# First MLP layer in seven half-block products for six pairs of feature blocks, positions worked parity by parity

## The chip, the core and the metric

The kernel runs on one core of a Trainium2 chip. The metric is the time of one execution on the device in microseconds (us), as the median of the runs of a kernel. A profile of one execution shows what each engine did: PE is TensorE (matrix products), DVE is VectorE, ACT is ScalarE, POOL is GpSimd, SP issues transfers (DMAs).

## The reference

A gated mix of two branches over 2048 positions of width 640: attention over eight positions at a distance of two (32 heads of 20 features), and an MLP with Mish of inner width 1728. Both read the same `x`.

```python
g = _sigmoid((x * gate_w).sum(-1, keepdims=True))
# branch A: idx = pos - 2 * (0..7), masked below 0
qkv = x @ wqkv
logits = jnp.einsum("bhsd,bhswd->bhsw", q, kg) * scale
o = jnp.einsum("bhsw,bhswd->bhsd", _softmax(logits), vg)
a = o @ wo
# branch B
h = jnp.einsum("bsd,df->bsf", x, w1) + b1
act = h * jnp.tanh(softplus(h))
b = jnp.einsum("bsf,fd->bsd", act, w2)
return g * a + (1 - g) * b
```

## The kernel before

**Precision and products.** Every fp32 operand is split into a high part (a copy on ACT, L373) and a low part (a subtraction on DVE or POOL, L376), and every product is three matmuls into one accumulation in a PSUM bank (`mm3`, L405 to L410): high by high, high by low, low by high. A split tile is called `pair`. There are seven banks for products, and an eighth, `side`, for the attention.

**Tiling.** Positions are laid out as 128 partitions by 16 slots. A slot belongs to one of two parities P (a window reaches back in steps of two, so attention stays in one parity), and the 2048 positions form four token blocks `tb` of 512, two for each parity. The width of 640 is five chunks `kc` of 128. The 1728 features of the MLP are 13 blocks `fc` of 128 and a rest of 64.

**First stage.** Eight units u = (quarter of the heads, parity), parity changing fastest, each make q, k and v for eight slots of 128 positions (`qkv`, L568): 15 matmuls of 496 columns for a slot. The result goes by ACT (`qkv_evac`, L558: L561, L563, L565) from the bank to one of two buffers, `kvq0` and `kvq1` in turn, the last unit to a third, `kvq2`, where six tiles of `x` lay before. Between the units stand the 52 blocks of the first MLP layer (`mlp1`, L698): for one feature block and one token block, 15 matmuls of 512 columns into a bank, then bias and Mish on ACT (L670), then stores to DRAM.

**Attention.** It runs on DVE (`attention`, L441), unit after unit, in two halves of four slots: scores (L461, L464), softmax (its exponential on ACT, L486), weighted sum (L503 to L512), and a turn (L416, `ot`) that ends the half. A buffer `kvq` may be overwritten by the unit after next only behind the turn of its half (`freed`). ACT copies q to `side` ahead of the scores (L467).

**Second stage.** The second MLP layer (`mlp2`, L869) is already made of seven products, a, b, c, e, g, d, f, over token-block pairs and weight sums. Behind product a its four `p` banks are copied by ACT (`copy`, L885) to places in `kvq1`, which is allowed only when the attention of unit 5 is over (`free5`); product b then goes on accumulating in the same banks, and its first matmul into each must wait for the copy. Then `wo_out` multiplies the attention's output by `wo`; its last part, chunks 3 and 4 of token blocks 2 and 3, is 60 matmuls.

**Order.** A list scheduler (`Plan`, L59) walks through all tasks with a cost for each, and writes one fixed instruction order for each engine. Tasks marked "ANY" (low parts of splits, sums) go to POOL or DVE; DVE takes one when PE needs it soon (`due`, L120). PE's tasks keep the order in which they are added. On the chip each engine works through its order strictly, and waits on semaphores.

## Time and profile before

| | |
|---|---|
| median of 3 runs | 637.5 us (635.89 to 637.86) |
| the profiled execution's own time | 636.0 us |
| its span, first to last instruction | 634.2 us |
| instructions | 8574 |
| moved by DMA | 136.49 MB, mean 215 GB/s |
| HBM read, written | 76.85 MB, 57.02 MB |

The span is what the profile divides up; 1.8 us of the execution's own time lie around it. A busy share is an average over stages with different limits, so a change is judged in the stage that it touches: the first stage runs to about 400 us, the second to the end.

### The profile page before, as it was taken

Reading aid. Unit: us, or ns where it says so; the run is one execution under the profiler, and the core shown is the slowest. Engines: PE = TensorE matmul, PEld = TensorE weight load, DVE = VectorE, ACT = ScalarE, POOL = GpSimd, SP = SyncE. Lnnn points to the kernel's source line nnn. Section 1 sums busy time; section 2 is a strip of 40 time slices with the busy share of each in tenths; the row PEclk is TensorE's granted clock in tenths of the full one; section 3 lists DMA queues with packets and bytes.
Section 4 is the critical chain, followed back from the end, with each engine's and each line's share of the span. In section 5 each row is a group of like instructions: output and inputs, shape, how many; then the busy total and the mean of one; then the engine's idle time right before and its main releaser. Section 6 shows DMA issues by size and latency. Waiting matters only on the chain.

```text
span 634.2 us, 8574 instructions
## 1 busy us (share of the span) xinstructions
PE 628.9 (99%) x2789; PEld 523.3 (83%) x2789; DVE 535.4 (84%) x524; ACT 334.2 (53%) x744; POOL 187.9 (30%) x179
## 2 busy tenths in 40 slices
PE   9999999999999999999999999999999999999997
PEld 6888888888888888888888888888888888888885
DVE  6589969999996999999799879999999999984230
ACT  7785753436436432443634245765687645674224
POOL 2667334333203230222242224444315613000000
PEclk9999999999999999999999999999999999999999
DMA  8999999859923994699499936898988677976204
GB/s 318 380 329 188 269 166 289 246 147 288 253 76 94 276 237 89 200 203 206 93 276 232 215 81 188 247 260 235 303 272 303 201 225 233 269 263 211 84 0 166
DMA packets 91085, 136.49 MB, mean 215 GB/s; under 512 B 12176, under 2 KB 41232, under 8 KB 91008
## 3 DMA queue, kind: packets, MB, share of 16 engines
q1 hardware_dynamic: 83360, 122.04, 62.2%
q0 software_dynamic: 7680, 13.90, 14.7%
q8 instruction: 22, 0.36, 0.2%
q14 instruction: 23, 0.19, 0.1%
HBM read 76.85 MB, written 57.02 MB: 211 GB/s over the span
## 4 chain that ended last, share of the span: by engine, by line
PE 97%; DMA 1%; ACT 1%; POOL 0%; issue 0%; DVE 0%; SPq 0%; ACTq 0%
PE bank L410 32%; PE bank L409 32%; PE bank L408 32%; PE bank L555 1%; DMA b<-kvq 1%; PE bank L357 1%; POOL pair L376 0%; PE bank L987 0%; PE bank L986 0%; ACT kvq L885 0%; ACT bank L885 0%; ACT kvq L1061 0%; DVE lg L353 0%; SPq L382 0%; ACTq L1061 0%
## 5 line engine op out<-in xcount | busy, mean ns | idle before, releaser
L409 PE MATMUL bank<-pair 128*128 128x512 f32 (+1 forms) x460 | 177.6, 386 | 0.1
L410 PE MATMUL bank<-pair 128*128 128x512 f32 (+1 forms) x460 | 177.5, 386 | 0.0
L408 PE MATMUL bank<-pair 128*128 128x512 f32 (+1 forms) x460 | 177.5, 386 | 0.0
L376 POOL TENSOR_TENSOR pair<-raw,pair 128x512 fp32r<-128x512 f32 (+2 forms) x47 | 58.7, 1266 | 148.2 <-ACT pair L373 39.8
L409 PEld LDWEIGHTS bank<-pair 128*128 128x128 f32 x460 | 86.3, 188 | 17.1 <-POOL pair L376 0.5
L408 PEld LDWEIGHTS bank<-pair 128*128 128x128 f32 x460 | 86.3, 188 | 16.5
L461 DVE TENSOR_TENSOR pr<-kvq,side 128x2560 f32<-128x2560 f32 x32 | 90.2, 2818 | 11.6 <-ACT side L467 11.2
L410 PEld LDWEIGHTS bank<-pair 128*128 128x128 f32 x460 | 86.3, 188 | 16.4
L499 DVE TENSOR_TENSOR pr<-kvq,side 128x2560 f32<-128x2560 f32 x32 | 90.3, 2820 | 1.1
L464 DVE TENSOR_REDUCE lg<-pr 128x128 f32<-128x2560 f32 x32 | 90.2, 2818 | 0.9
L561 ACT ACTIVATE kvq<-bank 128x320 f32<-128x320 f32 x64 | 28.2, 441 | 114.0 <-PE bank L410 114.0
L373 ACT ACTIVATE pair<-raw 128x512 fp32r<-128x512 f32 (+2 forms) x113 | 66.1, 612 | 13.6 <-DMA raw<-actt 8.5
L408 PE MATMUL bank<-pair,kvq 128*128 128x512 f32 (+1 forms) x188 | 72.6, 386 | 0.0
L409 PE MATMUL bank<-pair,kvq 128*128 128x512 f32 (+1 forms) x188 | 72.6, 386 | 0.0
L410 PE MATMUL bank<-pair,kvq 128*128 128x512 f32 (+1 forms) x188 | 72.6, 386 | 0.0
L670 ACT ACTIVATE hb<-bank,bias 128x512 f32<-128x512 f32 x52 | 35.8, 688 | 67.5 <-PE bank L410 59.2
L408 PE MATMUL bank<-pair,w 128*128 128x512 f32 x182 | 70.8, 389 | 0.0
L409 PE MATMUL bank<-pair,w 128*128 128x512 f32 x182 | 70.8, 389 | 0.0
L410 PE MATMUL bank<-pair,w 128*128 128x512 f32 x182 | 70.8, 389 | 0.0
L376 DVE TENSOR_TENSOR pair<-raw,pair 128x512 fp32r<-128x512 f32 (+2 forms) x66 | 46.9, 725 | 18.9 <-ACT pair L373 18.9
L658 POOL DMA_DIRECT2D actt<-actt x28 | 25.6, 964 | 87.3 <-issue 25.5
L509 DVE TENSOR_TENSOR pr<-pr 128x1280 f32<-128x1280 f32 x32 | 49.5, 1547 | 0.9
(103 smaller groups left out, 923.0 us busy)
## 6 DMA issues: line engine op xcount, KB each, us to landing
actt<-hb SPq DMA_DIRECT2D x52, 256.0 KB, 4.8
act<-hb SPq DMA_DIRECT2D x38, 256.0 KB, 4.1
raw<-actt SPq DMA_DIRECT2D x31, 256.0 KB, 4.1
raw<-act SPq DMA_DIRECT2D x27, 256.0 KB, 4.0
actt<-hb POOLq DMA_DIRECT2D x26, 256.0 KB, 6.4
actt<-actt POOLq DMA_DIRECT2D x24, 256.0 KB, 5.7
hb<-actt SPq DMA_DIRECT2D x23, 256.0 KB, 3.6
kvq<-in_xt SPq DMA_DIRECT2D x16, 320.0 KB, 7.1
```

What stands on the lines that cost most here:

```text
L373: a = add("ACT", act_ns(n), lambda: A.activation(hi(), raw(), AF.Copy), after, rank=rank, take=take, hold=hold)
L376: return (V if e == "DVE" else G).tensor_tensor(lo(), raw(), hi().bitcast(F32), op=OP.subtract)
L408: nc.tensor.matmul(ps, ah, bh, start=first, stop=False, skip_group_check=more)
L409: nc.tensor.matmul(ps, ah, bl, start=False, stop=False, skip_group_check=more)
L410: nc.tensor.matmul(ps, al, bh, start=False, stop=last, skip_group_check=more)
L461: return V.tensor_tensor(pr, window(kv, s0, 0), qs[:, :, None, :].to_broadcast([128, 2, W, QF]), op=OP.mult)
L464: return V.tensor_reduce(lg_w[:, s0:s0 + 2], pr.rearrange("p s w (h d) -> p s w h d", d=DH), op=OP.add, axis=AX.X)
L499: return V.tensor_tensor(pr.rearrange("p s w (h d) -> p s w h d", d=DH), vw, pw[:, :, :, :, None].to_broadcast([128, 2, W, HQ, DH]), op=OP ...
L509: step("DVE", 1495, lambda: V.tensor_tensor(pr[:, :, 0:4], pr[:, :, 0:4], pr[:, :, 4:8], op=OP.add))
L561: a = add("ACT", 330, lambda: A.activation(kv[:, 7 + s], ps.t[:, QF:3 * QF].rearrange("p (a b) -> p a b", a=2), AF.Copy), [done] + before, ...
L658: return add("POOL", 1200, lambda: G.dma_start(out=blk[key][:rows], in_=src(), accum_op=OP.add, max_dma_last_dim=2048), after, rank=-0.5, ...
L670: a = add("ACT", 595, lambda: A.activation(to(it()), src(), AF.Mish, bias=bias[:n, fc:fc + 1]), after + [bias_in], rank=NEXT, take=[] if h ...
```

## The change

Feature blocks q and q + 7 (q from 0 to 5) are taken together with the two token blocks of a parity, and chunks 0 to 3 of the width in two halves: two by two blocks, whose product takes seven half products instead of eight (the Winograd form of Strassen's). The fifth chunk is multiplied as before and added to the same banks. Feature block 6 stays as it was (`mlp1`).

- `quad(q, P, R)` does one such group on PE: 14 chunk products and 4 for the fifth chunk, 54 matmuls, where four calls of the old `mlp1` make 60. Five banks are used; shared part sums go from bank to bank, and to a tile `z`, by ACT (`copy` in `quad`, four a group). The two blocks of feature q + 7 are ended on DVE by adding `z` to the bank (`closed`, two a group), and Mish then reads the tile.
- `sums_of_x(P)` loads eight tiles of `x` again, makes four sums of tokens for each half and splits them. `weights_of(q, again)` makes the sums of weights, stores them, and for parity 1 loads and splits them again.
- Units are now u = 4 P + quarter: all of parity 0, then all of parity 1. `wq` is loaded and split for each parity anew, `x` of parity 1 comes only with its units (`x2`, `y3`).
- The order of PE's work is a string, `FRONT` for the first stage and `BACK` for steps inside `mlp2` (sums of `w2`, the rest of the features, gates, `wo`). Splits of `wo` go to `pair` tiles. In the scheduler POOL may begin work when DVE is free, and ACT puts off an exponential while a group is open.

In the order of PE 2800 rows become 2728 (one row a matmul; nine loads, and one branch, belong to the start).

```diff
+SIZES = {"pair": 23, "home": 6, "raw": 9, "hb": 4, "z": 2}
+FRONT = """q1 s0 w0 Q00 Q01 Q10 F0 r00 F1 Q11 g1 r10 T00 q2 T10 r20 Q20 r30 T20 r40 Q21 q3 T30 T40 Q30 r50
+w1 y3 q4 T50 x2 s1 Q31 F2 r01 Q40 M0 M1 F3 T01 S0 r11 r21 T11 q5 r31 Q41 T21 Q50 r41 S3 S1
+q6 T31 S2 Q51 T41 Q60 r51 T51 Q61 q7 H S4 Q70 Q71"""
+BACK = "40W 37P0 39P1 48P4 19G 4S6 0M2 0M3 0S5"
...
-                        if on:
+                        if on and busy["DVE"] and now < quiet:
+                            fit = [t for t in fit if t.kind != "plus" or now - t.rdy > self.STAY] or fit
+                        if on and busy["DVE"]:
...
+                        if self.open > 0:
+                            fit = [t for t in fit if t.kind != "exp" or now - t.rdy > self.HELD]
...
+    def sums_of_x(P):
+        early = EARLY_S * P
+
+        t0, t1 = 2 * P, 2 * P + 1
+        for kp in range(2):
+            raws = {}
+            for tb, kc in ((t1, 2 * kp), (t1, 2 * kp + 1), (t0, 2 * kp), (t0, 2 * kp + 1)):
+                raws[tb - t0, kc - 2 * kp] = raw = raw_buf()
+                raw.ready = [dma(lambda raw=raw: raw.t, lambda tb=tb, kc=kc: x[tb, kc], take=[raw])]
...
+            s1 = sum_into((a22, 0), (a21, 0), (a22, 0), OP.add, a21.ready + a22.ready + a22.read, 512, early=early)
+            s3 = sum_into((a21, 0), (a11, 0), (a21, 0), OP.subtract, [s1] + a11.ready + a21.read, 512, early=early)
+            s2 = sum_into((a11, 0), (a22, 0), (a11, 0), OP.subtract, [s3] + a11.read, 512, early=early)
+            s4 = sum_into((a12, 0), (a12, 0), (a11, 0), OP.subtract, [s2] + a12.ready + a12.read, 512, early=early)
+            for i, raw, t in ((1, a22, s1), (2, a11, s2), (4, a12, s4), (3, a21, s3)):
+                XS[kp, i] = halved(raw, [t], home_buf() if i < 4 else None)
...
+    def weights_of(q, again):
+
+        fa, fb = q, q + KH
...
+        if again:
+            return [load_pair(lambda: w1[fa][:, :4], "ANY", cols=4)] + [load_pair(lambda i=i: t_d[q, i], "ANY", after=t_in[q, i]) for i in range(1, 4)]
...
+        s1 = sum_into((r[2], 0), (r[1], 0), (r[0], 0), OP.subtract, [d0, d1], 256, take=[r[2]])
+        d3 = add("SP", 900, fifth, [s1], take=[r[3]], size=131072)
+        s2 = sum_into((r[2], 256), (r[1], 256), (r[2], 0), OP.subtract, [s1], 256)
+        s3 = sum_into((r[1], 0), (r[1], 256), (r[1], 0), OP.subtract, [s2], 256)
+        s4 = sum_into((r[3], 0), (r[0], 256), (r[2], 256), OP.subtract, [s2, d3], 256)
...
+    def quad(q, P, R):
+
+        fa, fb, t0, t1 = q, q + KH, 2 * P, 2 * P + 1
+        one, five, two_, three, four = ps_buf(), ps_buf(), ps_buf(seeded=True), ps_buf(seeded=True), ps_buf(seeded=True)
+        z5, z12 = z_buf(), z_buf()
...
+        p1 = mm(one, of(xs(t0, 0), 0, 0), [], True, True, [one], "open")
+        p5 = mm(five, of(s(1), 2, 0), [p1], True, True, [five])
+        c2 = copy(two_, one, [p1])
+        c5 = copy(z5, five, [p5])
+        p6 = mm(two_, of(s(2), 2, 256), [p5, c2])
+        p2 = mm(one, of(xs(t0, 1), 0, 256) + [(X[t0, 4], R[3], 256)], [p6, c2], False, True)
+        mish(lambda: one.t, 128, fa, t0, [p2], [one])
+        c3 = copy(three, two_, [p6])
+        p7 = mm(two_, of(s(3), 1, 0), [p2, c3])
+        c4 = copy(four, two_, [p7], "shut")
+        p3 = mm(three, of(s(4), 1, 256) + [(X[t0, 4], R[3], 384)], [p7, c3], False, True)
+        p4 = mm(two_, of(xs(t1, 1), 3, 0) + [(X[t1, 4], R[3], 256)], [p3, c4], False, True)
+        p8 = mm(four, [(X[t1, 4], R[3], 384)], [p4, c4], False, True)
...
+        a = closed(three, z12, [p3, c5], [z12])
+        mish(lambda: z12.t, 128, fb, t0, [a], [], home=z12)
+        a = closed(four, z5, [p8, c5, a])
+        mish(lambda: z5.t, 128, fb, t1, [a], [], home=z5)
```

What this does to the order of the engines is shown at three places.

DVE, the rows up to the turn that ends the second half of unit 4 (`side` is the bank with q and the weights, `pr` the scratch tile of the attention, `kvq_219` and `kvq_220` are `kvq0` and `kvq1`). Before:

```order
L461 TENSOR_TENSOR pr<-kvq_220,side 128x2560
L464 TENSOR_REDUCE lg<-pr 128x2x8x8
L503 TENSOR_TENSOR side<-lg,sm 128x2x8x8
L499 TENSOR_TENSOR pr<-kvq_219,side 128x2560
L509 TENSOR_TENSOR pr<-pr 128x2x640
L510 TENSOR_TENSOR pr<-pr 128x2x320
L512 TENSOR_TENSOR kvq_219<-pr 128x320
L416 STREAM_TRANSPOSE ot<-kvq_219 128x4x5x32
```

The same place now:

```order
L488 TENSOR_TENSOR pr<-kvq_220,side 128x2560
L491 TENSOR_REDUCE lg<-pr 128x2x8x8
L860 TENSOR_TENSOR z<-bank_69,z 128x512
L860 TENSOR_TENSOR z<-bank_63,z 128x512
L530 TENSOR_TENSOR side<-lg,sm 128x2x8x8
L526 TENSOR_TENSOR pr<-kvq_219,side 128x2560
L536 TENSOR_TENSOR pr<-pr 128x2x640
L537 TENSOR_TENSOR pr<-pr 128x2x320
L539 TENSOR_TENSOR kvq_219<-pr 128x320
L443 STREAM_TRANSPOSE ot<-kvq_219 128x4x5x32
```

The attention's steps are the same, and the two additions that close a group stand between them (L860); elsewhere splits stand there.

ACT, where the first bank of the second half of unit 6 is taken from PSUM (`hb` and `z` hold results of the MLP, the brackets name the engines and queues whose semaphores are waited for). Before:

```order
L670 ACTIVATE hb<-bank_68,bias 128x512 [waits DMASW7_49]
L561 ACTIVATE kvq_219<-bank_69 128x320 [waits PE_49]
L563 ACTIVATE kvq_219<-bank_69 128x160
L565 ACTIVATE hx<-bank_69 128x16
L561 ACTIVATE kvq_219<-bank_64 128x320 [waits PE_49]
L563 ACTIVATE kvq_219<-bank_64 128x160
```

Now:

```order
L704 ACTIVATE z<-z,bias 128x512 [waits DVE_49]
L911 ACTIVATE raw<-raw 128x128 [waits DMAHW5_49,Pool_49]
L394 ACTIVATE pair<-raw 128x512 [waits DMAHW2_49]
L394 ACTIVATE pair<-raw 128x512 [waits DMAHW5_49,PE_49]
L587 ACTIVATE kvq_219<-bank_64 128x320 [waits DVE_49,PE_49]
L589 ACTIVATE kvq_219<-bank_64 128x160 [waits DVE_49]
```

The step that waited for PE alone now waits for DVE as well: by its count for the row L537 above, and the row L589 behind it for the turn.

ACT, where the banks of product a are copied. Before:

```order
L760 ACTIVATE pair<-raw 128x384 [waits DMAHW2_49,PE_49,Pool_49]
L673 ACTIVATE w<-w 64x512 [waits Activation_49]
L885 ACTIVATE kvq_220<-bank_69 128x512 [waits PE_49]
L885 ACTIVATE bank_68<-kvq_220 128x512 [waits Activation_49]
L885 ACTIVATE kvq_220<-bank_64 128x512 [waits PE_49]
```

Now:

```order
L911 ACTIVATE raw<-raw 128x128 [waits DMAHW4_49,Pool_49]
L394 ACTIVATE pair<-raw 128x512 [waits DMAHW0_49,PE_49]
L1046 ACTIVATE kvq_220<-bank_64 128x512 [waits DVE_49,PE_49]
L1046 ACTIVATE bank_63<-kvq_220 128x512 [waits Activation_49]
L1046 ACTIVATE kvq_220<-bank_68 128x512 [waits PE_49]
```

Here too a wait for DVE has come in, by its count for the split that stands just ahead of the last two sums (L537, L539) and the turn of unit 5's second half. In the order of PE, 42 matmuls stand between the last one of product a into this bank and the first one of product b into it, before and now.

More of the change, by code (lines that the diff above doesn't have):

```diff
@@ L130, in fits @@
                 if b.ring.free < want[b.ring] or b.ring.line[b.ring.at + want[b.ring] - 1] is not b:
+                    return False
+                if b.can and not b.can():
                     return False
@@ L268, in ps_buf @@
         b.gone = lambda: unused.append(at[0])
+        if seeded:
+            b.can = lambda: any(i in whole for i in unused)
         return b
@@ L371, in split @@
     def split(raw, hi, lo, n, after, eng, hold, take=(), rank=SOON):
-        a = add("ACT", act_ns(n), lambda: A.activation(hi(), raw(), AF.Copy), after, rank=rank, take=take, hold=hold)
+        a = add("ACT", act_ns(n), lambda: A.activation(hi(), raw(), AF.Copy), after, rank=rank, take=take, hold=hold, kind="hi")
         def low(e=eng):
@@ new lines, in mlp1, with sum_into, run @@
+        xs = [X[tb, kc] for kc in range(KC)] + [wide_, last_]
+        t = pe_add(15 * mm_ns(512), run, sum((b.ready for b in xs), []), take=[ps], hold=xs)
+        mish(lambda: ps.t, 128, fc, tb, [t], [ps])
+    def sum_into(to, x, y, op, after, n, take=(), early=0):
+        def run(e):
+            (t, i), (a, j), (b, k) = to, x, y
+            return (V if e == "DVE" else G).tensor_tensor(t.t[:, i:i + n], a.t[:, j:j + n], b.t[:, k:k + n], op=op)
+        return add("ANY", either("ANY", n), run, after, rank=SOON, take=take, hold=[to[0], x[0], y[0]], early=early)
@@ L728, in sums_of_w2 @@
     def sums_of_w2(kc):
[L730 removed]
+        a1, a2, apart = [raw_buf() for _ in range(3)]
         def halves(half, b):
@@ L1126, with w_all @@
-    counts = [8, 8, 9, 9, 9, 9]
-    for u in range(8):
-        hq, P = divmod(u, 2)
-        if P == 0 and hq:
-            for kc in range(KC):
-                wq_in(hq, kc, "ANY")
-        if u == 7:
-            break
-        qkv(u, P, hq)
-        if u < 6:
-            more(counts[u])
+    R = {}
+    def w_all(q, P):
+        R[q, P] = weights_of(q, P == 1)
+    gate_dots(0, X[1, 1].ready[0])
     def third():
```

360 lines of the change are left out of this document (218 added, 142 removed).

## The prediction

> **What bounds the kernel now.** I read the page first, its busy line and its chain that ended last.
>
> ```profile
> PE 628.9 (99%) x2789; PEld 523.3 (83%) x2789; DVE 535.4 (84%) x524; ACT 334.2 (53%) x744; POOL 187.9 (30%) x179
> PE 97%; DMA 1%; ACT 1%; POOL 0%; issue 0%; DVE 0%; SPq 0%; ACTq 0%
> ```
>
> PE is busy for 628.9 of 634.2 us, and 97% of the chain is PE. Busy alone would not do, since ends of matmuls are modelled, so I asked who waits for whom. The columns are the wait in total, how often, and the longest.
>
> ```profile
> ACT kvq L561 <- PE bank L410: 114.0, 53, 3.3
> ACT hb L670 <- PE bank L410: 59.2, 33, 2.7
> ```
>
> ACT waits for PE by more than 170 us, and among the sixty longest waits there is none of PE for another engine. So PE sets the end. Whether it goes on doing so depends on the engine with the next largest share, DVE, and DVE has to be read by stages: busy time and number of instructions of PE, PEld, DVE, ACT and POOL in each stretch, then the granted clock, the DMA share and GB/s.
>
> ```profile
> 0.00:75.00 75.00, 73.79 (x320) 60.02 (x321) 59.94 (x58) 56.58 (x133) 41.41 (x36) 1.00 1.02 300
> 75.00:400.00 325.00, 325.00 (x1458) 273.38 (x1457) 295.42 (x243) 144.59 (x363) 93.91 (x99) 1.00 0.77 193
> 400.00:550.00 150.00, 149.90 (x661) 123.80 (x661) 146.74 (x173) 96.21 (x185) 52.60 (x46) 1.00 0.84 254
> 550.00:634.00 84.00, 80.23 (x354) 66.08 (x353) 33.28 (x53) 36.86 (x66) 0.00 (x0) 1.00 0.46 156
> ```
>
> From 75 to 400 us DVE idles 325.0 - 295.4 = 29.6 us; from 400 to 550 only 3.3 us, and yet PE loses 0.1 us there. A DVE that is 98% full can keep PE fed, but it has nothing to spare. What ends DVE's idle time between 75 and 400 us, and between 400 and 550 us:
>
> ```profile
> DVE sm L491 <- ACT lg L486: 11.7, 3, 6.1
> DVE pr L461 <- ACT side L467: 11.2, 4, 6.0
> DVE side L503 <- ACT side L467: 0.3, 1, 0.3
> ...
> DVE w L416 <- DMA actt<-w: 0.7, 1, 0.7
> DVE pair L761 <- ACT pair L760: 0.7, 1, 0.7
> DVE pair L376 <- ACT pair L373: 0.4, 2, 0.3
> ```
>
> In the first stretch 23.2 us are named waits, for an exponential or for the next unit's q; in the second 1.8 us.
>
> **What the change takes from PE.** Matmuls of 512 columns follow each other at 149.90 us / 661 = 0.2268 us (row 400 to 550; the 0.39 us of one in the groups is its length, which overlaps the next). Twelve groups of 54 replace twelve of 60, so 72 matmuls go: 72 x 0.2268 = 16.3 us. All lie in the first stage, where PE has no gap, so the profiled execution's own time of 636.0 would become 619.7 us if nothing else came to hold PE.
>
> **What it adds to DVE.** The groups by form, with mean ns of one:
>
> ```profile
> L376 DVE TENSOR_TENSOR pair<-raw,pair 128x512 fp32r<-128x512 f32 x57 | 42.1, 750 | 18.9 <-ACT pair L373 18.9
> L376 DVE TENSOR_TENSOR pair<-raw,pair 128x496 fp32r<-128x496 f32 x2 | 1.4, 676 | 0.0
> L1064 DVE TENSOR_TENSOR kvq<-bank,kvq 128x512 f32<-128x512 f32 x5 | 3.5, 691 | 6.7 <-PE bank L410 6.7
> L743 DVE TENSOR_TENSOR raw<-raw 128x256 f32<-128x256 f32 x10 | 5.9, 591 | 0.0
> L761 DVE SCALAR_TENSOR_TENSOR pair<-raw,pair 128x384 fp32r<-128x384 f32 x6 | 3.3, 553 | 0.7 <-ACT pair L760 0.7
> ```
>
> And some of them line by line: minimum, median and maximum ns, first and last start.
>
> ```profile
> L376 DVE TENSOR_TENSOR pair<-raw,pair x66: 413/684/3524, 8.2 to 590.6; 128x512 fp32r<-128x512 f32 x57, 128x384 fp32r<-128x384 f32 x6, 128x496 fp32r<-128x496 f32 x2, 128x256 fp32r<-128x256 f32 x1
> L376 DVE TENSOR_TENSOR w<-raw,w x8: 816/818/2198, 12.7 to 277.8; 128x640 fp32r<-128x640 f32 x8
> L416 DVE STREAM_TRANSPOSE ot<-kvq x16: 834/846/848, 78.5 to 544.8; 128x640 f32<-128x640 f32 x16
> L416 DVE STREAM_TRANSPOSE w<-hx x4: 401/437/445, 378.5 to 411.7; 128x256 f32<-128x256 f32 x4
> ```
>
> The place that counts is the twelfth turn, which ends unit 5. In DVE's order 295 instructions lead up to it before, now 359. The difference by kinds, at medians where there are some: 34 more splits and sums of 512 columns (0.684: 23.3 us), 24 closing additions from a bank (nearest row L1064, 0.691: 16.6), 12 splits of 496 (0.676: 8.1), 2 of 384 (0.553: 1.1), 2 turns of the rest (0.437: 0.9), 2 sums of 256 fewer (0.591: -1.2), 8 splits of 640 fewer (0.818: -6.5). That is 42.3 us more DVE work ahead of unit 5's end. Behind it DVE has 222 instructions in place of 229, so no more than before. The attention's 90 us for each of its three large steps are untouched.
>
> **What it adds elsewhere.** ACT gets 120 more steps of 512 columns and 20 of 496, less 18 of 640 and 2 table loads, at
>
> ```profile
> L373 ACT ACTIVATE pair<-raw 128x512 fp32r<-128x512 f32 x82 | 50.3, 628 | 10.0 <-DMA raw<-actt 8.5 <-DMA raw<-act 1.0 <-DMA raw<-o 0.2
> L670 ACT ACT_TABLE_LOAD x13 | 16.7, 1283 | 0.2
> L376 POOL TENSOR_TENSOR pair<-raw,pair 128x512 fp32r<-128x512 f32 x25 | 32.8, 1317 | 79.0 <-DVE side L503 18.4 <-ACT pair L373 15.6 <-DMA raw<-in_wo 15.4
> L885 ACT ACTIVATE bank<-kvq 128x512 f32<-128x512 f32 x8 | 4.8, 600 | 1.9 <-DVE hb L889 1.4 <-DVE raw L889 0.4
> ```
>
> about 72 us: 334 becomes some 406 of 625, not a bound. POOL gets 61 more of 512 columns and some 23 sums: 188 becomes about 280, hidden beside DVE's large steps. DMA carries some 20 MB more (x, wq and weight sums twice) by 99 more issues on SP, nearly all before 400 us: 60 GB/s on top of 193 at a share of 0.77; the first row shows 300 at 1.02, so it stays below full, and I cost it at nothing; if loads come late, that falls into the upper bound below.
>
> **The new waits.** ACT now waits for DVE where it takes unit 6's banks and where it copies product a. ACT is in order: behind a waiting step stand the high parts of splits that PE needs next. I price the copy, where the dates can be had:
>
> ```profile
> 393.77 0.84 DVE L416 STREAM_TRANSPOSE ot<-kvq 128x640 f32<-128x640 f32 x1
> ...
> L885 ACT ACTIVATE kvq<-bank x24: 581/598/600, 415.9 to 562.3; 128x512 f32<-128x512 f32 x24
> ```
>
> Before, the twelfth turn starts at 393.8 and the first copy at 415.9: 22 us of slack. Now the copy is due at 415.9 - 16.3 = 399.6, and PE has 42 matmuls (9.5 us) until it needs the result: 409.1. The turn comes at 393.8 + 42.3 less the idle time that the new work fills. **Bounds:** nothing is filled (436.1) or all 29.6 us (406.5). I take the rate of the full stretch, 1.8 us of named waits in 150, so 3.9 in 325: 23.2 - 3.9 = 19.3 us are filled, and the turn starts at 416.8. My reason is that the waits for q arise because PE makes q late, which turns round, and that in all 16 halves there are now two large steps (5.6 us) between the subtraction and the sum behind the exponential, where two halves had none. The awaited step ends 1.3 us ahead of the turn (L510 and L512 lie between, 0.82 and 0.49), the copy takes 0.6: PE waits for 416.8 - 1.3 + 0.6 - 409.1 = 7.0 us. Unit 6's banks give the same lag earlier, not a second one: what PE lost once, DVE has gained. By the bounds it is 0 (negative, so no wait) to 26.3 us.
>
> **Copies inside a group.** The second bank is seeded while PE does the fifth product: 6 x 0.2268 = 1.36 us for a copy of 0.60 behind at most one step of 0.69 (Mish). Cost: nothing. With a table load ahead, 1.2 us, twelve times: 14.5 us at most.
>
> **Two rules.** A split on DVE took 3.524 us at worst against a median of 0.684, while POOL worked; the large steps with an operand in `side` do not show it:
>
> ```profile
> L461 DVE TENSOR_TENSOR pr<-kvq,side x32: 2806/2820/2823, 38.3 to 495.3; 128x2560 f32<-128x2560 f32 x32
> ```
>
> The Trainium skill, SBUF — State Buffer, section "Who interferes with whom", says that a DVE instruction with two SBUF inputs and a GpSimd instruction that reads SBUF exclude each other for a whole instruction. The trace agrees (3.524 us). As a mechanism of this kernel: splits of 512 cost 0.750 in the mean, 0.066 over the median; POOL's additions go from 112 to 196, so 0.116 each, and DVE would lose some 6 us more: rival three.
>
> The first nine matmuls take 4.02 us together, 0.45 each:
>
> ```profile
> 1.21 4.02 PE L357 MATMUL bank<-lg 128*128 128x512 bf16 x9 [1.21 <-DVE lg L353]
> ```
>
> The Trainium skill, TensorE: Matmul & The Clock Gate, Part 1, says that PE falls to half clock after some 3.4 us without work and needs as long to recover. A single pause of 7.0 us would by that cost some 1.7 us more, an estimate from that page; no pause here is long enough to show it, and the sum goes without.
>
> **The sum.** 636.0 - 16.3 + 7.0 = 626.7. The median of the runs shown is 1.5 us above the profiled execution, so 628.2, rounded to **628 us**.
>
> **Rivals.** *One, PE is never held:* the turn comes by 410, because DVE finds work in all its gaps; for it speaks the stretch at 98%. 637.5 - 16.3 = 621.2 us. *Two, DVE's gaps stay, slower:* DVE is in order too, and the change puts exponentials off while a group is open (up to 16.2 us by the scheduler's constant), and its closings wait for PE; if DVE keeps its waits as before, the turn comes at 436.1, PE waits 26.3 us at the copies of product a, and the time is 647.5. It equals 637.5 when 10 us are filled. Against it: in none of the halves does the sum now follow the exponential at once. *Three, the shared port:* 6 us more on DVE, 634 us. *Four, a seeded bank is late in every group:* 621.2 + 14.5 = 635.7; against it, ACT is kept from exponentials there. That PE does not get shorter cannot be: its order has 72 rows fewer.
>
> **Chances.** Forecast (624 to 632) 0.45; rival one (below 624) 0.20; between 632 and 635.6, rival three above all, 0.12; within 0.3% of 637.5, which is about what a measurement can tell (635.6 to 639.4), rival four and a half-filled DVE, 0.10; slower, rival two, 0.13. So faster 0.77. The range leaves out most of rival two and a little at the bottom: 620.5 (the floor less the spread of runs) to 638.
>
> **What would show it.** PE: 2717 matmuls and a pitch of 0.227; its waits, new in the list, at product b behind ACT's copies (L1046) and near unit 6. DVE: about 572 us busy, over 95% from 75 us to the twelfth turn, which starts near 417. ACT: waits for DVE at L587 and L1046. If the twelfth turn comes before 410 and PE still has gaps, my place is wrong; if splits of 512 take over 0.85 in the mean, it is the port; if gaps stand ahead of the second sum of each group, the seeds.

## The result, and the profile after

The changed kernel takes **644.7 us** in the median of 4 runs (641.79 to 646.83), beside 637.68 of the kernel before on the same chip: ratio 1.0113, 95% interval 1.0068 to 1.0158. It is 1.1% slower, where 628 was forecast. The profiled execution took 645.23 us, with a span of 643.5.

The page of the changed kernel, its busy line and its chain:

```profile
PE 619.0 (96%) x2717; PEld 512.0 (80%) x2717; DVE 565.5 (88%) x581; ACT 395.5 (61%) x867; POOL 278.5 (43%) x263
PE 32%; DVE 8%; issue 2%; POOL 1%; ACT 0%; DVEq 0%; POOLq 0%; ACTq 0%
```

The 72 matmuls are gone, and the busy times are near the forecast ones (DVE 565 for 572, POOL 278 for 280, ACT 395 for 406). But PE is no longer the chain's 97%. The chain can be followed back only to 364 us: a wait of PE of 0.24 us at 434.5 leads over POOL into DVE's attention, and the large pauses lie ahead of that. The list of waits shows them; it has PE in it, which it had not before (us waited in all, times, longest):

```profile
PE bank L435 <- ACT pair L394: 11.0, 1, 11.0
PE bank L435 <- ACT bank L833: 5.3, 4, 3.2
PE bank L437 <- DVE pair L397: 2.7, 2, 1.9
```

No wait at L1046 (product a) is there. By stages (columns as in the prediction's table):

```profile
0.00:75.00 75.00, 69.59 (x300) 56.43 (x300) 59.71 (x57) 50.68 (x129) 39.44 (x36) 0.98 0.88 254
75.00:400.00 325.00, 310.01 (x1365) 257.79 (x1364) 303.95 (x277) 207.91 (x469) 172.03 (x168) 0.97 0.92 254
400.00:550.00 150.00, 149.75 (x662) 123.84 (x661) 146.02 (x165) 91.52 (x189) 61.57 (x55) 1.00 0.83 259
```

From 400 us on PE has no gap (662 matmuls in 150 us). It lost its time ahead of that: added up over the starts of successive matmuls, what is beyond 0.225 us each (where it is 0.075 or more) comes to 28.4 us, against 2.6 in the kernel before: 25.8 us. Without them the execution would have taken 645.2 - 25.8 = 619.4; the forecast gave 619.7 for the products alone. **The gain is there, and 26 us of new pauses take it back and more.** The largest stands where the first group of the second parity begins. PE there:

```profile
219.53 0.39 PE L437 MATMUL bank<-pair 128*128 128x512 f32 x1
230.92 0.79 PE L435 MATMUL bank<-pair 128*128 128x512 f32 x1 [11.00 <-ACT pair L394]
231.51 0.63 PE L436 MATMUL bank<-pair 128*128 128x512 f32 x1
234.02 0.80 PE L437 MATMUL bank<-pair 128*128 128x512 f32 x1 [1.88 <-DVE pair L397]
```

219.53 is the last matmul of block 6 (F3), 230.92 the first product of block 0 in the second parity (T01). Its weights wait for their high part on ACT. What ACT and POOL did meanwhile:

```profile
225.50 0.63 ACT L394 ACTIVATE kvq<-raw 128x512 fp32r<-128x512 f32 x1 [8.24 <-POOL raw L749]
...
230.26 2.17 ACT L394 ACTIVATE pair<-raw 128x512 fp32r<-128x512 f32 x4
```

```profile
215.21 0.90 POOL L692 DMA_DIRECT2D actt<-hb  x1 [8.48 <-DMA actt<-hb]
...
222.13 0.84 POOL L692 DMA_DIRECT2D actt<-actt  x1 [1.87 <-DMA actt<-hb]
...
223.94 1.53 POOL L749 TENSOR_TENSOR raw<-raw 128x512 f32<-128x512 f32 x1
```

Read from the bottom: a sum of x (L749) waits on POOL behind accumulating transfers (L692), and one of these waits 8.48 us until the store that it adds to has landed. ACT works in order, and the high part of that sum stands in front of the high part of the weights, whose load had been issued at 209.8. From 225.5 on ACT works without a gap, and still takes 5.4 us until PE can start: a table load, the Mish of block 6 and its negation, and high parts stand ahead of the weights. So some 6 of the 11.4 us are the wait for POOL's sum, and the rest is what ACT's written order has in front. No step here is slow; each waits for the head of another queue.

The second pause (68.26 to 71.89) stands inside the first group, ahead of its second sum:

```profile
66.81 1.57 POOL L660 TENSOR_TENSOR pair<-pair 128x640 f32<-128x640 f32 x1 [0.85 <-DMA pair<-in_xt]
```

```profile
68.41 0.74 ACT L661 ACTIVATE pair<-pair 128x640 f32<-128x640 f32 x1 [5.04 <-POOL pair L660]
...
71.26 0.57 ACT L833 ACTIVATE bank<-bank 128x512 f32<-128x512 f32 x1
```

ACT waits 5.04 us for POOL's gate product, which no product of PE needs, and PE's copy (L833) is behind it.

### The profile page after: what moved, and what is told of

The parts are those of the page before. It is cut to its first block, busy times and chain, and to the rows that moved or that the text cites. A ratio compares the mean times of both kernels' runs of the same rounds, so it can differ in the third digit from the quotient of the medians.

```text
span 643.5 us, 9039 instructions
## 1 busy us (share of the span) xinstructions
PE 619.0 (96%) x2717; PEld 512.0 (80%) x2717; DVE 565.5 (88%) x581; ACT 395.5 (61%) x867; POOL 278.5 (43%) x263
## 5 line engine op out<-in xcount | busy, mean ns | idle before, releaser
L435 PE MATMUL bank<-pair 128*128 128x512 f32 (+1 forms) x812 | 315.4, 388 | 11.0 <-ACT pair L394 11.0
L437 PE MATMUL bank<-pair 128*128 128x512 f32 (+1 forms) x812 | 315.2, 388 | 2.7 <-DVE pair L397 2.7
L436 PE MATMUL bank<-pair 128*128 128x512 f32 (+1 forms) x812 | 315.0, 388 | 0.2 <-POOL pair L397 0.2
L435 PEld LDWEIGHTS bank<-pair 128*128 128x128 f32 x812 | 153.0, 188 | 41.3 <-ACT pair L394 11.7
L437 PEld LDWEIGHTS bank<-pair 128*128 128x128 f32 x812 | 152.9, 188 | 33.9 <-DVE pair L397 4.3
L436 PEld LDWEIGHTS bank<-pair 128*128 128x128 f32 x812 | 153.1, 189 | 30.2 <-POOL pair L397 0.7
L397 POOL TENSOR_TENSOR pair<-raw,pair 128x512 fp32r<-128x512 f32 (+3 forms) x102 | 131.0, 1314 | 96.2 <-ACT pair L394 18.1
L394 ACT ACTIVATE pair<-raw 128x512 fp32r<-128x512 f32 (+2 forms) x197 | 115.6, 609 | 43.2 <-DMA raw<-act 16.0
L526 DVE TENSOR_TENSOR pr<-kvq,side 128x2560 f32<-128x2560 f32 x32 | 90.2, 2819 | 0.8
L397 DVE TENSOR_TENSOR pair<-raw,pair 128x512 fp32r<-128x512 f32 (+3 forms) x95 | 61.6, 669 | 7.2 <-ACT pair L394 7.0
L692 POOL DMA_DIRECT2D actt<-actt x28 | 23.3, 830 | 64.4 <-DMA actt<-actt 35.0
L435 PE MATMUL bank<-kvq,pair 128*128 128x512 f32 x72 | 29.5, 409 | 5.3 <-ACT bank L833 5.3
L833 ACT ACTIVATE bank<-bank 128x512 f32<-128x512 f32 x36 | 20.9, 580 | 18.3 <-PE bank L437 18.3
L437 PE MATMUL bank<-kvq,pair 128*128 128x512 f32 x72 | 29.2, 406 | 0.0
L436 PE MATMUL bank<-kvq,pair 128*128 128x512 f32 x72 | 29.1, 404 | 0.0
L749 DVE TENSOR_TENSOR raw<-raw 128x512 f32<-128x512 f32 (+1 forms) x18 | 14.8, 824 | 15.3 <-DMA raw<-in_x 7.6
L749 POOL TENSOR_TENSOR raw<-raw 128x256 f32<-128x256 f32 (+1 forms) x22 | 18.9, 868 | 21.4 <-DVE raw L749 8.0
L537 DVE TENSOR_TENSOR pr<-pr 128x640 f32<-128x640 f32 x32 | 27.4, 857 | 0.6
(114 smaller groups left out, 639.6 us busy)
```

The costliest lines, as they stand in the source:

```text
L394: a = add("ACT", act_ns(n), lambda: A.activation(hi(), raw(), AF.Copy), after, rank=rank, take=take, hold=hold, kind="hi")
L397: return (V if e == "DVE" else G).tensor_tensor(lo(), raw(), hi().bitcast(F32), op=OP.subtract)
L435: nc.tensor.matmul(ps, ah, bh, start=first, stop=False, skip_group_check=more)
L436: nc.tensor.matmul(ps, ah, bl, start=False, stop=False, skip_group_check=more)
L437: nc.tensor.matmul(ps, al, bh, start=False, stop=last, skip_group_check=more)
L526: return V.tensor_tensor(pr.rearrange("p s w (h d) -> p s w h d", d=DH), vw, pw[:, :, :, :, None].to_broadcast([128, 2, W, HQ, DH]), op=OP ...
```

## The experiments

Five theories are told apart. **A**: steps that wait for POOL, or for a transfer through POOL, stand at the head of in-order queues. **B** and later **D**: DVE is too full, as forecast. **C**: the parity order itself. **E**: any other order brings new pauses. Every result is the median, with the ratio to the kernel before on the same chip and its 95% interval. The runs were made on several chips, so gains between them are taken from the distance to the kernel before on the same chip, which is 7.0 us for the changed kernel (644.7 - 637.7). Where a kernel moves or drops instructions "with all orders alike", every engine's order is otherwise that of the changed kernel.

**First four: take one suspect away.** The edits:

```diff
# e1
-    lambda: G.dma_start(out=blk[key][:rows], in_=src(), accum_op=OP.add, ...)
+    lambda: None if key in (("t1", 0, 5), ("t3", 0, 5), ("t2", 0, 5)) else G.dma_start(...)
# e2: L660 and L661 issue nothing for the second parity, zt[:, 1] = 0
# e3, in sum_into
+    if early: return add("DVE", dve_ns(n), lambda: run("DVE"), ...)
# e4 ("s" and "r" load x and w1 plainly, without sums)
-    "T": lambda q, P: quad(q, P, R[q, P])
+    "T": lambda q, P: [mlp1(f, tb) for f in (q, q + KH) for tb in (2 * P, 2 * P + 1)]
```

> The changed kernel with three of POOL's accumulating transfers left out (t1, t3 and t2 of block 5, first parity; all orders otherwise alike, three sums in memory are not made). Theory A (POOL's queue): in the changed kernel POOL waits 8.48 and 1.87 us for stores that these three add to, with a sum of x behind them that ACT, DVE and PE wait for. Without them that sum is some 9 us earlier, the pause of 11.4 us at 219.5 falls to 2 to 3, and the 23 matmuls at 0.43 behind it go back to 0.225 (4.8 us): 645.2 - 9 - 4.8 = 631, between 628 and 634. Theory B (DVE is full, as I forecast): DVE has not a step less; what PE gains at 219 it waits for at the copies of product a (L1046), whose first one starts in the same 0.1 us as the twelfth turn (427.8): 638 to 645. Theory A2 (the sum is late because its operands are): the pause stays over 8 us, 642 or more.

> The changed kernel without the eight gate products of the second parity (POOL L660 and ACT L661; the gate of that parity becomes a constant; their loads stay). Theory A (a step that waits for POOL stands in ACT's queue ahead of a copy that PE needs): ACT waits 5.04 us at 68.4 and 1.60 at 137.0 for POOL's product, with the copy between two products (L833) behind it. Without them the pauses of 3.63 and 1.71 us go, and the eight matmuls at 0.43 behind the first: 3.4 + 1.5 + 1.6 = 6.5 us, 638.7 (637 to 640.5); the pause at 219.5 stays at 11.4. Theory A3 (the copies are late for PE's own sake, the seed hidden too little): the pauses stay over 1 us, 643 or more. Theory B: the gain comes back at L1046, 644.

> The changed kernel with the eight sums of x of the second parity bound to DVE instead of left to DVE or POOL. Nothing is left out. Theory A: no sum of x stands behind an accumulating transfer; the pause at 219.5 goes down to 0 to 3 us at the price of one more step of 0.66 us on DVE: 628 to 634. Theory B: DVE is full, so the sums come late there, the pause stays over 5 us or returns at L1046: 638 to 648.

> The changed kernel with the parity order, its two loads of x, weights and q kept, but each of the twelve groups computed as four plain blocks of 15 matmuls (2789 again), with no sums and no copies between products. Theory A: the loss needs sums of x behind POOL's queue and copies in the middle of a group; both are gone, PE's gaps stay under 3 us, 636 to 640, so that the products alone are worth 16 us where nothing pauses. Theory C (the parity order and its extra loads make the loss): PE still pauses for 8 us or more at the change of parity, 644 to 655.

- e1: 639.6 us, 1.0031 [0.9999, 1.0063]. The pause of 11.4 became 5.0, the one of 2.5 stayed. The kernel is 2.4 us above the one before, in place of 7.0: some 5 of the 14 us hoped for.
- e2: 644.0 us, 1.0112 [1.0052, 1.0173]. The pause at 68 went from 3.6 to 1.0, and the slow matmuls behind it went; the one at 137 stayed at 1.4, so the gate product was not what set that one, and pauses of 1.2 us came at 107 and 113. The time is that of the changed kernel (1.0113), not the 638.7 expected.
- e3: 645.7 us, 1.0114 [1.0078, 1.0149]. At the change of parity 5.5 and 3.2 us are left, and new ones of 2.9 and 2.3 us come at 279 and 334. Moving the sums to DVE only moves the waits.
- e4: 649.6 us, 1.018 [1.0137, 1.0223]. No pause above 0.5 us at the change of parity, so that one does need the sums; but 2.3 us at 170, and 5.3 and 2.8 us at 470, where ACT waits 8.5 us for DVE with high parts behind. Neither A (636 to 640) nor C as stated (a pause at the change of parity) came out. The parity order with eight products has its own pauses.

**Second four: the sums gone, and three other orders.**

```diff
# e5, in sum_into
+    if early: return None
# e6, in FRONT
- M0 M1 F3 T01 S0 r11 r21 T11 q5 r31 Q41 T21
+ M0 M1 F3 Q41 T01 S0 r11 r21 T11 q5 r31 T21
# e7, in gate_dots: ACT's step
-    rank=NEXT if P else -0.2, hold=of(i)
+    rank=NEXT if P else -0.2, hold=of(i), late=4000 if P else 0
# e8: e6 and e7
```

> The changed kernel with the eight sums of x of the second parity left out (all orders otherwise alike; the products of that parity use rows of x that were not summed). Theory A now reads: at 219.5 PE waits for the high part of block 0's weights, which were loaded long before; it stands in ACT's queue behind a high part of a sum of x, and that sum stands in POOL's queue. With the sums gone nothing late is left in front: the pause of 11.4 us falls below 1, the one of 2.5 behind it too, the 23 matmuls at 0.43 go: 645.2 - 11 - 2.3 - 4.8 = 627 (624 to 631). Theory A4 (buffers or loads of the second parity are late by themselves): 4 us or more of the pause stay, 633 to 640. Theory B: the gain comes back as waits at the copies of product a, 638 to 645.

> The changed kernel with one move in the written order: the second half of unit 4's q, k and v (Q41, 60 matmuls of 496) stands ahead of the first group of the second parity instead of two groups behind it. Nothing is left out. Theory A: PE gets 60 x 0.22 = 13.2 us of other work while the sums of x are made, more than the pause of 11.4: 645.2 - 18.3 = 627 (624 to 633). Theory B (DVE is full): unit 4's second half arrives earlier, but DVE has the same work ahead of the twelfth turn; PE waits at product a instead, 634 to 645.

> The changed kernel with ACT's step on each gate product of the second parity put 4 us further back in the schedule. Nothing is left out. Theory A: ACT no longer waits 5.04 us for POOL's product in front of the copy inside the first group; the pause of 3.63 us at 68 and eight slow matmuls go (5 us): 640 (637 to 643), with the pause at the change of parity as it was, 9 to 12 us. If pauses are a matter of the whole schedule and not of this place, others come up and the time stays at 643 to 648.

> Both moves of the two runs before together, nothing left out. Theory A: 645.2 - 18.3 - 5 = 622 (619.5 to 629), below the kernel before by 2%. Theory B: 634 or more.

- e5: 641.3 us, 1.0088 [1.0055, 1.0122]. 3.9, 4.1 and 1.6 us stay at the change of parity: even without the sums something there is late (A4, half). The 3.9 us are the pause for weights that e12 takes apart below, and ahead of the next one ACT does wait for two loads of weight sums (0.35 and 0.97 us).
- e6: 655.4 us, 1.0293 [1.0275, 1.0312]; e7: 655.5, 1.0307 [1.029, 1.0324]; e8: 641.8, 1.0082 [1.0042, 1.0122]. In these three the scheduler lays out everything behind the edit anew, and pauses come at other places. Theory A as a theory of two places falls here. In e7 the forecast's own place appears for once, PE at product b behind ACT's copy of product a:

```profile
PE bank L435 <- ACT kvq L1046: 3.9, 1, 3.9
```

  But not for the turn: ACT's copy stands behind high parts that wait for loads there.

```profile
426.99 0.63 ACT L394 ACTIVATE pair<-raw 128x512 fp32r<-128x512 f32 x1 [1.68 <-DMA raw<-act]
...
427.94 0.58 ACT L1046 ACTIVATE kvq<-bank 128x512 f32<-128x512 f32 x1
```

**Third four: all of A's causes, and all of D's, with all orders alike.** So that no new order clouds the answer, kernels now drop instructions and keep every order.

```diff
# e9, in outputs (L536)
-    step("DVE", 1495, lambda: V.tensor_tensor(pr[:, :, 0:4], pr[:, :, 0:4], pr[:, :, 4:8], op=OP.add))
+    step("DVE", 1495, lambda: None)
# e10: every accumulating transfer (L692) issues nothing
# e11: e10, e2 and e5 together
# e12: e11 and e9
```

> The changed kernel without the first of the three folding additions of each attention half (L536, 32 x 1.49 us of DVE, 24 of them ahead of the twelfth turn: 35.8 us; the outputs are folded from half of the products). All orders otherwise alike. So far each pause that was taken away came back elsewhere, so two theories are left. Theory D (DVE and what runs in step with it are late everywhere, and the pauses are where that lateness meets PE): with DVE's work ahead of the twelfth turn back near that of the kernel before, PE's pauses fall from 26 to under 8 us, 621 to 628. Theory A (POOL's queue waits for stores, whatever DVE does): the pauses at 68 (3.6 and slow matmuls) and at 219 (over 8 of 11.4) stay, 636 to 643.

> The changed kernel without any of POOL's accumulating transfers (70 of them; sums in memory are not made). All orders otherwise alike. Theory A: POOL never waits for a store; the pause at 219 falls by 6 to 10 us and what is behind it, the one at 68 stays for its late load: 633 to 638. Theory D: what PE gains there it loses where DVE is awaited, above all at the copies of product a (twelfth turn near 422): 638 to 643.

> The changed kernel without POOL's accumulating transfers, without the gate products of the second parity and without the sums of x of the second parity (constants and rows that were not summed in their places). All orders otherwise alike, DVE's attention whole. Theory A: nothing is left in POOL's and ACT's queues that waits for a store or a late load; PE's pauses fall under 8 us, 621 to 628. Theory D: DVE is 5 us lighter at most, its twelfth turn comes near 418 and PE waits there; 630 to 640.

> Both at once: what the two runs before leave out, together. Both theories: PE's gaps stay under 5 us, 619 to 623, the floor of 636.0 - 16.3 us. If more than 8 us of gaps stay, a third cause (late loads, or the copies between products) is open.

- e9: 639.3 us, 1.0045 [1.0001, 1.0088]. The stage from 75 to 400 us, of e9 and then of e11 (third time in the row: DVE):

```profile
75.00:400.00 325.00, 315.78 (x1393) 263.09 (x1392) 290.17 (x266) 212.09 (x483) 179.39 (x175) 0.98 0.96 261
```

```profile
75.00:400.00 325.00, 317.64 (x1402) 264.26 (x1401) 308.68 (x287) 207.11 (x472) 121.79 (x115) 0.98 0.74 225
```

With 36 us less work ahead of the twelfth turn DVE idles 35 us in this stage, and the pauses stand where they stood: 4.7 us at 69, and 7.6 (for 11.4) and 2.5 at the change of parity. The gain is 3.8 us, with an interval that overlaps that of the changed kernel.

- e10: 638.3 us, 1.0037 [1.0019, 1.0056] (56 transfers by the trace, not 70). e11: **632.6 us**, 0.9947 [0.9928, 0.9966], with DVE at 308.68 of 325 us, fuller than in e9 or in the changed kernel. So D falls: with DVE as full and the queues clear, the kernel is 3.5 us below the kernel before in place of 7.0 above, a gain of 10.5, and lightening DVE on top (e12: 630.2, 0.9902 [0.9877, 0.9928]) gives 2.4 us. In e11 no wait of PE on L1046 shows.
- One rival these runs do not separate. Leaving out the accumulating transfers clears POOL's queue, but it also takes their traffic away: from 75 to 400 us the DMA share falls from 0.92 to 0.72 (e10) and 0.74 (e11), and weights (`raw<-in_w` of 256 KB) land in a median of 3.3 us in place of 5.6. So the gains of e10 to e12 are those of clear queues and of quicker transfers together. Only for the largest pause is the order shown by itself, by e13 below: there the DMA share stays at 0.93.
- But the 619 to 623 of both theories for e12 did not come: 9.3 us stay between 180 and 245 us. What they are, on ACT and then on PE in e12:

```profile
216.57 0.69 ACT L704 ACTIVATE hb<-bank,bias 128x512 f32<-128x512 f32 x1 [0.88 <-PE bank L437]
217.29 0.63 ACT L707 ACTIVATE hb<-hb 128x512 f32<-128x512 f32 x1
217.82 0.61 ACT L394 ACTIVATE kvq<-raw 128x512 fp32r<-128x512 f32 x1
218.34 0.61 ACT L394 ACTIVATE pair<-raw 128x512 fp32r<-128x512 f32 x1
218.86 0.61 ACT L394 ACTIVATE kvq<-raw 128x512 fp32r<-128x512 f32 x1
219.38 2.17 ACT L394 ACTIVATE pair<-raw 128x512 fp32r<-128x512 f32 x4
```

```profile
216.14 0.39 PE L437 MATMUL bank<-pair 128*128 128x512 f32 x1
220.05 0.79 PE L435 MATMUL bank<-pair 128*128 128x512 f32 x1 [3.52 <-ACT pair L394]
```

ACT's written order has the Mish of the block that PE has just ended (it waits for PE) in front of the weights that PE needs next (PE waits for it). So a pause of some 3.5 us comes from the written order, with the queues clear; e17 tests this by moving the Mish.

**Last six: the places moved by hand, no other order changed, and but for e17 everything computed.** An instruction is issued some steps of its engine later than the scheduler says (line numbers below are 18 to 57 higher, since lines were added: L412 is L394, L415 is L397, L544 is L526, L716 is L692, L864 and L890 are L833, L512 is L494):

```diff
# e13: t1, t3, t2 of block 5 are issued right behind the sum of x on POOL
# e14: ACT's gate steps (six of eight) are issued 14 ACT steps later, with the loads that reuse their buffers
# e15: e13 and e14
# e16: e15, and Mish, negation and store of (block 6, tb 3) behind the next seven high parts
# e17: e11, the move of e16, and one large step (L526) on DVE behind the next two low parts
# e18: e16, and that move of L526
```

> The changed kernel with three of POOL's accumulating transfers (t1, t3, t2 of block 5, first parity) moved behind the sum of x that stood behind them; every other instruction of every engine stays where it is in its engine's order, and nothing is left out. Theory A: as without them (639.6): the pause at 219.5 goes from 11.4 to about 5, 638 to 641. Theory E (any change of order brings a new pause elsewhere, as in the three runs where the scheduler was given another number): 643 to 655.

> The changed kernel with six of ACT's eight steps on the gate products of the second parity moved 14 of ACT's steps further back, behind the copies between products, and the six loads that reuse their buffers with them on SP; every other order stays, nothing is left out. Theory A: PE's pause of 3.6 us at 68 and eight slow matmuls go, the one at 137 in part; that at 219 stays at 11: 640 (638 to 642). Theory E: 643 to 655.

> Both moves of the two runs before, nothing left out. Theory A: 645.2 - 5 - 5.5 = 634.5 (632 to 637), PE's gaps from 30 to 180 us 3 to 4 us in all, from 180 to 245 us 9 to 10. Theory E: 640 or more.

> As before it, and also the Mish and the negation of block 6's last token block, with their store, moved on ACT behind the seven high parts that followed them; nothing left out. In the run with all queues clear PE still paused for 3.9 us at 216, from the end of that block over its Mish (0.69) and negation (0.63) and four high parts (0.53 each) to its own next weights, and for 2.5 us more for a low part behind a large step on DVE. Theory A: the first of these falls by 1.3 to 3 us, the second may stay: 632 (628 to 635). If the sums of x themselves, not ACT's order, set the end of that pause, it stays and the time is that of the run before, 634.5.

> The run with all queues clear (no accumulating transfers, no gate products and no sums of x of the second parity) and two moves of order at the change of parity: on ACT the Mish and negation of block 6's last token block behind the seven high parts that followed them, on DVE one large step (L526) behind the two low parts that followed it. In the run without these moves PE lost 9.2 us between 180 and 245 us, in pauses of 3.9 and 2.5 and the slow matmuls behind them. Theory A: both pauses fall under 1 us and the slow matmuls go: 632.6 - 8 = 624.5 (622 to 627), what then is over the floor of 619.7 is the start and 3 us of small pauses. If late loads or buffers are behind these pauses, 3 us or more of each stay: 629 or more.

> Everything computed; the three moves of the run called e16 and the large step on DVE behind two low parts. There PE paused for 3.7 us at 217.5 (a sum of x on POOL, two on DVE and three high parts in front of its weights), 2.7 at 221.8 (a low part behind the large step) and 2.8 at 227.6 (a low part of a sum of x on POOL, behind an add). Theory A: the second goes, 2.5 us and some slow matmuls: 636 (633 to 639), about the kernel before. If the first and third are set by the sums of x as a chain, they stay, and with them the change is worth nothing.

- e13: 642.7 us, 1.0091 [1.0058, 1.0123], where 638 to 641 was expected. The sum of x (L777 here) now starts at 219.2 in place of 223.9, and the pause goes from 11.4 to 5.0, just as in e1, with nothing left out: here the order alone makes the difference. But 1.8 us at 232 are new, for a low part of a sum that now stands on POOL behind the moved adds and one more, and 1.9 at 274, and in the time no gain is clear of the noise. POOL in e13:

```profile
219.21 1.31 POOL L777 TENSOR_TENSOR raw<-raw 128x512 f32<-128x512 f32 x1
...
226.50 0.84 POOL L716 DMA_DIRECT2D actt<-actt  x1 [4.28 <-DMA actt<-hb]
231.89 0.81 POOL L716 DMA_DIRECT2D actt<-actt  x1 [4.55 <-DMA actt<-actt]
232.45 1.56 POOL L415 TENSOR_TENSOR kvq<-raw,kvq 128x512 fp32r<-128x512 f32 x1
```

- e14: 641.9 us, 1.0077 [1.0052, 1.0102]. The pause at 68 falls only to 2.7 (at 73). With the gate step out of the way, the next head of ACT's queue waits for DVE, and the second copy (L864) still stands behind it:

```profile
69.14 0.61 ACT L864 ACTIVATE bank<-bank 128x512 f32<-128x512 f32 x1
73.35 0.44 ACT L512 ACTIVATE side<-kvq 128x320 f32<-128x320 f32 x1 [3.60 <-DVE pr L544]
73.72 0.58 ACT L864 ACTIVATE z<-bank 128x512 f32<-128x512 f32 x1
```

- e15: 642.0, 1.0076 [1.0047, 1.0105]: the pauses are 17.4 us from 30 to 245 us, against 25.2 in the changed kernel, where 13 were expected.
- e16: 639.6 us, 1.0043 [1.0014, 1.0071]; e18: 639.0, 1.0032 [1.0005, 1.0059]. The pause of 11.4 is down to 3.7, but what is next now shows. The 632 us expected of e16 did not come, and in e18 the second pause at the change of parity, which was to go, is still 2.3 us. PE's waits in e16:

```profile
PE bank L453 <- ACT bank L890: 3.4, 4, 1.6
PE bank L453 <- ACT pair L412: 3.3, 1, 3.3
PE bank L454 <- POOL kvq L415: 2.4, 1, 2.4
PE bank L455 <- DVE pair L415: 2.1, 1, 2.1
```

  Copies and weights on ACT, a low part of a sum on POOL, a low part on DVE: the queues of three engines, 2 to 3 us each. No version that computes everything beat the kernel before.
- e17: **630.0 us**, 0.9894 [0.987, 0.9918]. The first pause is gone (0.2 us), as A has it; 1.6 and 3.0 us are left for low parts on DVE:

```profile
217.47 1.77 DVE L415 TENSOR_TENSOR pair<-raw,pair 128x512 fp32r<-128x512 f32 x1
219.16 2.81 DVE L544 TENSOR_TENSOR pr<-kvq,side 128x2560 f32<-128x2560 f32 x1
```

  The first took 1.77 us itself, where 0.68 is usual. POOL worked on a split of its own at the same time:

```profile
217.01 1.67 POOL L415 TENSOR_TENSOR kvq<-raw,kvq 128x512 fp32r<-128x512 f32 x1 [3.38 <-DVE kvq L415]
```

  The others stand behind the large step, which only changed its place. So what sets these two is the next steps on DVE, and not a late load. 624.5 was expected.

The pauses of PE in the profiled execution of each, worked out as above for stretches from 30 us on (the first 30 us have 1.8 to 2.7 us in each), and the start of the twelfth turn:

```
                        own time   30-180  180-245  245-400  400-end   12th turn
before                   636.0       0        0        0       0.4      393.8
changed                  645.2       8.6     16.6      0.9     0.5      427.8
e9   DVE lighter         640.6       8.2     12.0      0       0.8      421.7
e10  no adds             638.8       9.4     10.3      0       0        418.1
e11  queues clear        632.9       3.3      9.2      0       0        412.3
e17  and two orders      631.0       5.0      6.2      0       0        410.6
e7   gate step later     654.6       3.9      8.3      2.4    19.9      425.3
e16  three moves         638.9       5.7     12.2      0.4     1.2      421.5
```

## Why the prediction was wrong, step by step

**The 72 matmuls, 16.3 us: right.** The execution less its new pauses is 619.4, forecast 619.7.

**DVE's added work, 42.3 us: right; what follows from it: wrong.** The stretch from 75 us to the twelfth turn, before and then changed:

```profile
75.00:393.77 318.77, 318.77 (x1431) 268.19 (x1430) 289.22 (x237) 138.73 (x348) 89.94 (x95) 1.00 0.77 194
```

```profile
75.00:427.82 352.82, 337.83 (x1488) 280.93 (x1487) 331.16 (x302) 221.25 (x501) 187.54 (x182) 0.97 0.91 253
```

DVE is busy 331.2 - 289.2 = 41.9 us more. But its idle time fell only from 29.6 to 21.7 us: 7.9 were filled, not 19.3, and the turn came at 427.8, not 416.8. Part of that is PE's own doing, since DVE waits too at the change of parity (6.4 us for the sum on POOL). The price of the late turn, 7.0 us at product a, was not paid at all: by then PE was late itself, and the first copy (L1046, at 427.78) held nobody. Only e7 shows a wait there, 3.9 us, and that for loads.

**POOL's added work, "hidden beside DVE's large steps" and so without a term in the sum: this is the step that failed.** POOL's busy time was forecast to 2 us, and its 91 us more do lie beside DVE. But I priced busy time, and the cost is in what stands behind what: 25.8 us of pauses where the sum had 7.0, and those at another place. The accumulating transfers were on POOL before, as many as now (56, in these three rows), with about the same waits for stores (44.5 us in the first two rows, 51.3 now):

```profile
L658 POOL DMA_DIRECT2D actt<-actt x28 | 25.6, 964 | 87.3 <-issue 25.5 <-DMA actt<-actt 25.2 <-DVE pr L510 6.8
L658 POOL DMA_DIRECT2D actt<-hb x26 | 25.4, 977 | 27.3 <-DMA actt<-hb 19.3 <-ACT hb L670 6.4 <-ACT hb L673 1.6
L658 POOL DMA_DIRECT2D actt<-w x2 | 1.7, 844 | 0.7 <-ACT w L670 0.7
```

They cost PE nothing there: splits stood in the same queue, but no wait of PE for POOL is among the waits. The change put sums into it on which two more engines hang. An add cannot go earlier: the Trainium skill, DMA: Bandwidth & Descriptors, section "Rules for kernel authors", says that an accumulating transfer has to wait for the earlier transfer to the same bytes, since nothing holds them in between. The trace shows that wait with 8.48 us. By the distances to the kernel before, leaving out the adds gave 7.0 - 2.3 = 4.7 us, gate products and sums of x on top 5.8 (both on one chip), and the two orders on ACT and DVE 3.4 more (e17: 6.9 us below, where e11 has 3.5). The 11 us of pauses that e17 still has were not taken apart further; but for the two named there, what sets them is open.

**DMA, costed at nothing: right in the rate, open in the cost.** From 75 to 400 us the core moved 254 GB/s, where 193 + 60 was forecast, at a share of 0.92. But transfers land later than before: the stores `actt<-hb` in a median of 5.1 us (4.5 before), loads of `wq` in 5.4 (4.0). How much of the pauses this makes, no run shows.

**The change of parity was not a place of my forecast.** I followed the twelfth turn and product a, because DVE has the next largest share. But there is one point where the whole supply of PE (x, its sums, weights, q) is exchanged, and it was there to be seen in the written order: between F3 and T01 stand no other products of PE.

**Copies inside a group: forecast at nothing, measured 5.3 us.** Four of the 36 seeds were late, and 3.2 us of it is the one behind the gate step; in e11, without gate products, 1.2 us are left. Rival four, a late seed in every group, did not come.

**Rivals.** The sign is that of rival two, and its 647.5 us is close, but that is luck, since neither place nor cause is: DVE's gaps stayed in good part, yet lightening DVE by 36 us returned 3.8 us on its own and 2.4 where the queues were clear, while clearing the queues returned 10.5. Rival three is out as a cost of the change: the splits on DVE got cheaper, not dearer, with POOL half as busy again.

```profile
L397 DVE TENSOR_TENSOR pair<-raw,pair 128x512 fp32r<-128x512 f32 x75 | 50.0, 683 | 6.2 <-ACT pair L394 6.0
```

Before, 57 of them took 750 ns in the mean; now 683. Added up over all of DVE, what single steps take beyond the median of their kind (by more than 0.1 us) is 13.3 us before and 12.2 now. Single steps beside POOL are still long, and where PE waits for one, as in e17, it shows.

Theory E is half true, and it is why a better version was not found: three edits that made the scheduler lay out the rest anew gave 641.8 to 655.5 us, with pauses at places that no theory had named.

## What to carry to other kernels

Price an added instruction not by its time on an engine that has room, but by its queue: what in front of it can wait, for how long, and who waits for what stands behind. Where all inputs of the bound engine change at one point, write down for that point which of them is ready when, before looking at averages over a stage. To tell "too much work" from "wrong order", drop the suspect's instructions and keep every order; an edit that makes a scheduler plan anew changes both at once. Where the suspect is a transfer, dropping it takes its traffic away too; moving it, as e13 does, keeps the two apart.

## What the runs showed of the hardware

A pause costs more than its length. Behind the pause of 3.63 us at 68 the matmuls go on at 0.43 us each, eight of them, 1.6 us in all. In e4 a pause of 2.3 us is enough:

```profile
170.28 0.38 PE L437 MATMUL bank<-pair 128*128 128x496 f32 x1
172.58 0.49 PE L435 MATMUL bank<-pair 128*128 128x496 f32 x1 [1.91 <-ACT hx L591]
...
174.03 0.62 PE L435 MATMUL bank<-pair 128*128 128x496 f32 x1
174.44 0.62 PE L436 MATMUL bank<-pair 128*128 128x496 f32 x1
```

Eight matmuls follow there at 0.41. Over all runs, of the pauses that stand alone none up to 2.1 us had slow matmuls behind it; from 2.2 to 2.9 us 9 of 13 had (2.7 us in e3 had none), and where no further pause came between it was 7 or 8 of them, about 3 us at half pace, that is 1.5 us lost. The Trainium skill, TensorE: Matmul & The Clock Gate, Part 1, gives one idle window of some 3.4 us as the condition, in windows that run freely; the length of the slow stretch agrees with that window, the pause needed was shorter here. In the changed kernel there are 8 slow matmuls behind the pause at 68 and 12 behind those at the change of parity (not 23, as the expectations have it): 20 x 0.2 = 4 of the 26 us.
